# The last matrix product of a gated Fourier-mixing layer: the order of the first two units of each token block, and the memory order of two weight pieces

## The chip, the cores and the metric

One Trainium2 chip; the kernel runs on one of its cores. The metric is the device time of one execution in microseconds (us), taken as the median of several executions. Engines are called by short names: PE (TensorE: matrix products, PEld its weight loads), DVE (VectorE), ACT (ScalarE), POOL (GpSimd) and SP (SyncE, which here only issues transfers). Each engine runs its own instruction list in the order that the program wrote.

## The reference

With x of 2048 tokens by 512 features, all in 32-bit floats:

```
xn  = layernorm(x)
s   = Cseq_re @ (xn @ Cd_re.T) - Cseq_im @ (xn @ Cd_im.T)     # Fourier mixing: 2048x2048 and 512x512 matrices
h   = relu(xn @ w1 + b1) ** 2                                # 512 -> 1792
g   = silu(h @ w2 + b2)                                      # 1792 -> 512
out = x + s * g
```

The change lies in `h @ w2`, called MLP2 here.

## The kernel before, in words

**Precision and products.** Each 32-bit operand is split into a high half (HI, a rounded copy made by ACT, line 69) and a low half (LO, the remainder, subtracted by DVE, line 72), and each product is three passes: HI·HI, HI·LO, LO·HI (line 32). Matrix products of two-by-two blocks are done in the Winograd way, with seven products instead of eight (line 48). So before a product can run, its operands need sums of blocks (DVE, lines 201 to 209), then the two halves.

**Stages.** The Fourier mixing comes first; it fills the first 407 us of the span. Then MLP1 (`hidden`, line 525), and MLP2 (line 789 on). MLP1 and MLP2 are cut in 28 units each: four token blocks c = 0..3 of 512 tokens, by seven pieces p = 0..6 of the 1792 hidden features. A unit is numbered n = 7c + p; block 1 begins with unit 7, block 2 with unit 14, block 3 with unit 21. MLP1 writes each unit's h to memory (`hd`, line 557, issued on ACT's queue), and MLP2 reads it back (`hr`, line 569, on SP's queue).

**A unit of MLP2 on the engines.** `operand(n, c, p)` (line 560) loads `hr`, forms the sums on DVE (lines 207 to 209), then the HI half on ACT and the LO half on DVE into one of three places in turn (`sixth(2 + n % 3)`, line 579). `outer` (line 593) issues one product on PE: two columns of three passes, six matmuls of 128x256. A unit is seven products, 42 matmuls. In each product the first two matmuls use only the unit's HI half; the third uses its LO half.

**The weights.** w2's piece p, split and summed, has 2 halves x 7 slots x 256 columns for each partition. Pieces 0, 1 and 6 are made from w2 on the spot, late in the run. Pieces 2 to 5 lie ready in memory (`w2d`) and are loaded by `load_w2` (line 493) into places that MLP1's weights leave. Pieces 2 and 3 land where a neighbour's last 16 columns still lie, so each is loaded in two goes: "s" (slots 1 to 6 of both halves) and, when the neighbour is done, "f" (slot 0 of both halves). Piece 4 is loaded whole ("l").

**Accumulators (banks).** The seven products of a block add up in PSUM over the seven units. Products 2 and 6 share a two-bank tile, products 7, 5 and 3 a three-bank tile; 1 and 4 have a bank each. The two- and three-bank tiles are the same banks in every block, so the next block can start in them only when DVE has read out the previous block (`combine`, lines 234 to 243) and ACT has written the bias (line 591). Products 1 and 4 alternate between banks, which are free earlier. The first unit of a block therefore takes its products in the order 1, 2, 6, 4, 7, 5, 3 (`FIRST`, line 52), all other units in the order 1, 2, 6, 7, 5, 3, 4 (`ORDER`). Block 3 has an order of its own.

**What sets the order.** MLP1 and MLP2 are written under `tc.manual_schedule` (line 705): each engine executes in the order in which the Python code issues. In MLP2's loop (line 789), step n issues the products of unit n, then DVE's sums for unit n + 3, then, if it is a block's last unit, `combine`, and then the two halves of unit n + 2 (line 835) and the load of unit n + 6. So at the end of block 0 (step 6), DVE's list reads: sums of unit 9, `combine` of block 0, LO half of unit 8. In the same way the LO half of unit 15 follows `combine` of block 1.

**Counters.** A transfer tells of its landing on one of eight counters (DMAHW0 to DMAHW7), given out by the program; before a counter is used again, the issuing engine waits for the transfer that used it last.

Of the kernel before, what the change touches and what calls it, by code (L numbers as in the profile page):

```python
# [7 lines left out]
F32 = mybir.dt.float32  # L8
# [16 lines left out]
REST = NP - 3  # L25
# [24 lines left out]
ORDER = (1, 2, 6, 7, 5, 3, 4)  # L50

FIRST = (1, 2, 6, 4, 7, 5, 3)
FIRST_LAST = (1, 2, 5, 4, 6, 7, 3)
# [9 lines left out]
def fnet_gated_kernel(ctx, tc, x, xt, ct, wd, w1, w2, b1, b2, out):  # L63
    nc = tc.nc
# [22 lines left out]
    def bank(tag, name):  # L87

        n = {"b3": 3, "b2": 2}.get(tag, 1)
        return acc.tile([P, n, 512], F32, tag=tag, name=name)  # L90

    def buf(tag, shape, name, dtype=F32, bufs=1):
        return pool.tile(shape, dtype, tag=tag, bufs=bufs, name=name)
# [19 lines left out]
    def sixth(j, a, on=LINE):  # L113

        v = block[:, (7 - j) * 3584 + on:][:, 0:3584]
        return v.rearrange("p (a b n) -> p a b n", a=a, n=256)
# [189 lines left out]
    def load_rows(c, t):  # L306

        flat = rows.rearrange("a b -> (a b)")
        for m in range(2):
            for h in range(2):  # L310
                n = m * S + c * TC + h * 256
                nc.sync.dma_start(t[:, 2 * m + 1 - h], bcast(flat[n:n + 256], 256))
        xT["rows"] = t
# [138 lines left out]
    W1, W2, H, fin = {}, {}, {}, {}  # L452
# [3 lines left out]
    W2D = {p: dram.tile([P, 2, 7, 256], F32, name=f"w2d{p}") for p in range(NP) if p not in W2_DIRECT}  # L456
# [20 lines left out]
    def load_w1(p):  # L477
        if p < NP - 1:
            t = sixth(2 + p, 2)
            nc.sync.dma_start(t.bitcast(F32), W1D[p])  # L480
            W1[p] = [t[:, :, n] for n in range(7)]
        else:
            a = buf("g0b", [P, 2, 3, 256], f"w1a_{p}", F32R)
            b = buf("g1b", [P, 2, 4, 256], f"w1b_{p}", F32R)
            nc.sync.dma_start(a.bitcast(F32), W1D[p][:, :, 0:3])
            nc.sync.dma_start(b.bitcast(F32), W1D[p][:, :, 3:7])
            W1[p] = [a[:, :, n] for n in range(3)] + [b[:, :, n] for n in range(4)]

    W2_HOME = "xc0", "xc1", 5, 6, 7, "wd0", "wd1"

    FRACTION = {"l": slice(0, 7), "s": slice(1, 7), "f": slice(0, 1)}

    def load_w2(p, slots=slice(0, 7)):
        to = W2_HOME[p]
        if p not in W2:
            W2[p] = sixth(to, 2, 0) if p in (2, 3, 4) else buf(to, [P, 2, 7, 256], f"w2_{p}", F32R)
        nc.sync.dma_start(W2[p][:, :, slots].bitcast(F32), W2D[p][:, :, slots])

    def late_w2(p):

# [210 lines left out]
    def go(*names):  # L711


        for v in names:
            k, n = v[0], int(v[1:])
            if k == "m":
                load_rows(n, buf("pq00", [P, 4, 256], f"rows{n}"))
            elif k in FRACTION:
                load_w2(n, FRACTION[k])
            elif k != "h" or n < len(units):  # L720
                if v not in making:
                    making[v] = {"h": lambda: operand(n, *units[n]), "x": lambda: tokens(n // 2, n % 2),
                                 "w": lambda: late_w2(n)}[k]()
                next(making[v])
# [28 lines left out]
    c = NTC - 1  # L753
# [8 lines left out]
    with ordered:  # L762
        before = None
        for n, (c, p) in enumerate(units):
            ahead, behind = beside.get((c, p), ((), ()))
            go(*ahead)
            unit = hidden(n, c, p)
            next(unit)
            if n == 0:
                load_w1(5)  # L770
                load_w1(6)
            if n == len(units) - 1:

                m26, m4 = bank("b2", "m_b2_o0"), bank("ba", "m_ba_o0")
                bias(m26[:, 0], 2)
                bias(m4[:, 0], 4)
            if before:
                next(before)
            next(unit)
            go(*behind)  # L780
            before = unit
            if n == 0:
                stage2(NC - 1, 0)
                stage2(NC - 1, 1, "ba")
        m753, m1 = bank("b3", "m_b3_o0"), bank("bb", "m_bb_o0")
        bias(m753[:, 1], 5)
        next(before)

        for n, (c, p) in enumerate(units):
            last = c == NTC - 1  # L790
            if n == 0:
                ms = m26, m753, m4[:, 0], m1[:, 0]
                at_ = product
            elif not last and p == 0:

                m4, m26, m753, m1 = (bank(tag, f"m_{tag}_o{c}") for tag in (("bb", "ba")[c - 1], "b2", "b3", "bc"))
                ms = m26, m753, m4[:, 0], m1[:, 0]
                bias(ms[2], 4)
                bias(product(ms, 2), 2)
                bias(product(ms, 5), 5)  # L800
            elif p == 0:

                m5, m40 = (bank(tag, f"m_{tag}_last")[:, 0] for tag in ("bb", "bc"))
                m12, m67 = bank("b2", "m_12"), bank("b3", "m_67")
                m3 = bank("ba", "m_ba_last")[:, 0]
                m4 = m40, m67[:, 2]
                ms = {1: m12[:, 0], 2: m12[:, 1], 6: m67[:, 0], 7: m67[:, 1], 5: m5, 3: m3}
                at_ = dict.__getitem__
                bias(m5, 5)
                bias(m40, 4, slice(0, 1))  # L810
                bias(ms[2], 2)
                bias(m4[1], 4, slice(1, 2))

            def add(k, p):
                if last and k == 4:
                    for i in range(2):
                        outer(m4[i], k, ready[c, p], p, (i,))
                else:
                    outer(at_(ms, k), k, ready[c, p], p)

            go(*{0: ("l5",), 1: ("w6",)}.get(n, ()))
            if not last or p < REST:
                for k in ORDER if p else FIRST_LAST if last else FIRST:
                    add(k, p)
            if n == 1:

                nc.scalar.activation(stats[:, 0, 0, 0:1], stats[:, 0, 0, 0:1], AF.Silu)
            go(f"h{n + 3}")
            if p == NP - 1 and not last:
                e = buf("e", [P, 4, 512], f"z{c}")  # L830
                combine(e, ms)
                done_next = c, e
            if c and not last and p in (3, 4):
                put(*done, p - 1)
            go(f"h{n + 2}", *{2: ("w6",), 3: ("w6",)}.get(n, ()), f"h{n + 6}")
            if p == (3 if last else 5):
                load_fin(c)
            if p == NP - 1 and not last:
                done = done_next
            elif c:  # L840
                for k in ((2, 3), (0,), (1,), (), (), (), ())[p] if not last else ((), (0,), (1, 2), (3,), (), (), ())[p]:
                    finish(*done, k)


        e = buf("g1a", [P, 4, 512], f"z{c}")
        tail = NP - 1
        whole = slice(0, 512)
        w = [slice(i * 256, (i + 1) * 256) for i in range(2)]

        def rest(ks, ps=range(REST, NP)):  # L850
            for k in ks:
                for f in ps:
                    add(k, f)

        def step(to, a, b, op, w=whole):
            nc.vector.tensor_tensor(e[:, to, w], a[:, w], e[:, b, w], op=op)

        rest((1, 2, 6), range(REST, tail))
        rest((1, 2), (tail,))
        nc.scalar.activation(e[:, C21], ms[1], AF.Copy)  # L860
        step(C11, ms[2], C21, ALU.add)
        silu(e, C11)
        times(c, e, C11)
        plus(c, e, C11)
        rest((6,), (tail,))
        rest((7,))
        step(C22, ms[6], C21, ALU.add)
        step(C21, ms[7], C22, ALU.subtract)
        rest((5,))
        step(C12, m5, C22, ALU.subtract)  # L870
        step(C22, m5, C21, ALU.add)
        silu(e, C22)
        rest((3,))
        for f in range(REST, NP):
            outer(m4[0], 4, ready[c, f], f, (0,))
        times(c, e, C22)
        plus(c, e, C22)
        step(C12, m3, C12, ALU.add)
        silu(e, C12)
        step(C21, m4[0], C21, ALU.subtract, w[0])  # L880
        silu(e, C21, one)
        for f in range(REST, NP):
            outer(m4[1], 4, ready[c, f], f, (1,))
        times(c, e, C12)
        step(C21, m4[1], C21, ALU.subtract, w[1])
        silu(e, C21, two)
        times(c, e, C21, one)
        plus(c, e, C21, one)
        times(c, e, C21, two)
        plus(c, e, C21, two)  # L890
        plus(c, e, C12)
# [43 lines left out]
```

## Time and profile before

| | |
|---|---|
| median of 3 executions | 707.4 us (706.16 to 708.9) |
| the profiled execution | 707.11 us, of which 705.3 us are the span of its instructions |
| PE busy | 685.6 us, 97% |
| DVE busy | 583.9 us, 83% |
| ACT busy | 346.7 us, 49% |
| bytes moved | 141.09 MB, 200 GB/s mean |
| MLP2 on PE | from 553.18 us to the end |

Timeline rows read: start, length, engine, source line, operation, what it writes and reads, count; in brackets the engine's idle time just before and what ended it. `m_bb_o`, `m_b_o`, `m_ba_o`, `m_bc_o` are accumulator banks of MLP2; the `m_b_o` stand for both the two-bank and the three-bank tile. `block` is the large area that holds the units' halves and the weights. The views give line 598 for every product of MLP2 and line 72 for every LO half, so a unit is known by its place in the order.

### The profile page before, as it was taken

What the parts mean: (1) busy time and instruction counts of PE and PEld (TensorE: products, weight loads), DVE (VectorE), ACT (ScalarE), POOL (GpSimd) and SP (SyncE); (2) the same over time, 40 slices, a digit from 0 to 9 for tenths busy, and PEclk for the clock granted to TensorE, in tenths of its full rate; (3) what the DMA queues carried; (4) which work ended last, traced back from release to release, by engine and by line L of the source; (5) the groups of instructions that cost most, each with busy time, mean ns of one, the idle gap of its engine ahead of it and who ended that gap; (6) DMA issues with size and microseconds to landing.
All of it is one profiled execution on the core that took longest, in us unless ns stands there. A gap on an engine that the chain in (4) does not pass through costs nothing.

```text
span 705.3 us, 12798 instructions
## 1 busy us (share of the span) xinstructions
PE 685.6 (97%) x5179; PEld 646.1 (92%) x5179; DVE 583.9 (83%) x886; ACT 346.7 (49%) x475; POOL 5.2 (1%) x8
## 2 busy tenths in 40 slices
PE   8999999999999999999999999999999988999985
PEld 5778788999999999999999989999999988999985
DVE  7999654779599698797797756999999679999995
ACT  3447332444353544544452415777777744444531
POOL 0000000000000000000000000000000000101000
PEclk9999999999999999999999999999999999999999
DMA  9622441534563653835836976566737985777733
GB/s 323 229 90 91 153 131 46 196 119 141 203 226 135 221 200 119 299 132 179 293 99 251 357 299 210 207 234 216 269 122 235 356 334 180 194 224 193 248 125 123
DMA packets 55818, 141.09 MB, mean 200 GB/s; under 512 B 5072, under 2 KB 22224, under 8 KB 54736
## 3 DMA queue, kind: packets, MB, share of 16 engines
q1 hardware_dynamic: 50640, 124.56, 51.1%
q10 hardware_dynamic: 4032, 14.68, 5.2%
q0 software_dynamic: 1088, 1.05, 1.1%
q8 instruction: 40, 0.66, 0.4%
q14 instruction: 18, 0.15, 0.1%
HBM read 97.00 MB, written 43.27 MB: 199 GB/s over the span
## 4 chain that ended last, share of the span: by engine, by line
PE 73%; DVE 18%; DMA 4%; issue 2%; ACT 1%; SPq 0%; DVEq 0%; ACTq 0%
PE m_b L300 23%; PE yps L287 12%; PE hps L544 7%; PE m_b_o L598 7%; PE m_bb L300 5%; PE m_ba L300 5%; PE hps_b L544 4%; DVE block L72 4%; PE pq_b L353 3%; PE hps_ba L544 2%; DVE g L72 2%; DMA w2raw<-in_w 1%; DVE bn L133 1%; PE m_bc_o L598 1%; PE hps_bb L544 1%
## 5 line engine op out<-in xcount | busy, mean ns | idle before, releaser
L300 PE MATMUL m_b<-g,block 128*128 128x256 f32 x1080 | 129.1, 276 | 0.0
L300 PEld LDWEIGHTS m_b<-g,block 128*128 128x128 f32 x1080 | 125.5, 188 | 0.0
L69 ACT ACTIVATE g<-r 128x768 fp32r<-128x768 f32 (+2 forms) x65 | 57.3, 885 | 82.8 <-PE m_b L300 38.1
L72 DVE TENSOR_TENSOR g<-r,g 128x768 fp32r<-128x768 f32 (+2 forms) x65 | 65.4, 1007 | 35.3 <-ACT g L69 35.2
L287 PE MATMUL yps<-wd,pq 128*128 128x512 f32 (+1 forms) x414 | 92.9, 374 | 0.0
L287 PEld LDWEIGHTS yps<-wd,pq 128*128 128x128 f32 x414 | 74.8, 188 | 14.0
L72 DVE TENSOR_TENSOR g<-t,g 128x1024 fp32r<-128x1024 f32 x48 | 58.6, 1221 | 11.8 <-ACT g L69 11.8
L544 PE MATMUL hps<-xT,block 128*128 128x256 f32 x504 | 59.7, 277 | 0.7 <-DVE h L243 0.7
L544 PEld LDWEIGHTS hps<-xT,block 128*128 128x128 f32 x504 | 58.4, 188 | 1.0 <-PE hps L544 0.9
L69 ACT ACTIVATE g<-t 128x1024 fp32r<-128x1024 f32 x48 | 50.3, 1048 | 14.4 <-PE m_ba L300 6.5
L353 PE MATMUL pq_b<-g,block 128*128 128x512 f32 x180 | 47.6, 398 | 1.8 <-DVE g L72 1.7
L598 PE MATMUL m_b_o<-w,block 128*128 128x256 f32 x360 | 43.7, 277 | 2.6 <-ACT m_b_o L591 2.6
L555 ACT ACTIVATE h<-h,b1s 128x512 f32<-128x512 f32 x56 | 37.3, 715 | 17.3 <-DVE h L242 17.2
L300 PE MATMUL m_b<-g,xc 128*128 128x256 f32 x360 | 45.1, 277 | 0.0
L598 PEld LDWEIGHTS m_b_o<-w,block 128*128 128x128 f32 x360 | 42.0, 188 | 3.3 <-ACT m_b_o L591 3.2
L69 ACT ACTIVATE block<-hr 128x768 fp32r<-128x768 f32 (+1 forms) x28 | 35.5, 1269 | 18.6 <-DVE hr L209 7.7
L353 PEld LDWEIGHTS pq_b<-g,block 128*128 128x128 f32 x180 | 32.9, 188 | 11.3 <-DVE g L72 2.4
L300 PEld LDWEIGHTS m_b<-g,xc 128*128 128x128 f32 x360 | 42.9, 188 | 0.3
L72 DVE TENSOR_TENSOR block<-hr,block 128x768 fp32r<-128x768 f32 (+1 forms) x28 | 41.6, 1485 | 0.1
L201 DVE TENSOR_TENSOR t<-r 128x512 f32<-128x512 f32 x48 | 32.9, 685 | 4.9 <-DMA r<-in_ct 4.7
L544 PE MATMUL hps_b<-xT,block 128*128 128x256 f32 x288 | 34.7, 276 | 0.0
L544 PEld LDWEIGHTS hps_b<-xT,block 128*128 128x128 f32 x288 | 33.6, 188 | 0.0
(200 smaller groups left out, 1182.1 us busy)
## 6 DMA issues: line engine op xcount, KB each, us to landing
r<-in_ct SPq DMA_DIRECT2D x63, 512.0 KB, 3.6
hd<-h ACTq DMA_DIRECT2D x28, 512.0 KB, 4.7
hr<-hd SPq DMA_DIRECT2D x28, 512.0 KB, 4.9
w1d<-w0g SPq DMA_DIRECT2D x21, 512.0 KB, 3.2
block<-w1d SPq DMA_DIRECT2D x6, 1792.0 KB, 8.7
y<-ysb SPq DMA_DIRECT2D x16, 256.0 KB, 3.0
fin<-y SPq DMA_DIRECT2D x16, 256.0 KB, 4.8
out<-z SPq DMA_DIRECT2D x15, 256.0 KB, 4.0
```

What stands on the lines that cost most here:

```text
L69: nc.scalar.activation(hi, src, AF.Copy)
L72: return nc.vector.tensor_tensor(lo, src, hi.bitcast(F32), op=ALU.subtract)
L133: nc.vector.bn_stats(bn, t[:, h])
L201: nc.vector.tensor_tensor(t[:, 0:2], r[:, 0:1].to_broadcast([P, 2, 256]), r[:, 1:3], op=ALU.add)
L287: nc.tensor.matmul(ps[:, s], PQ[c, m, k // 2][:, a_, w:w + P], WD[m, k][:, b_, s], start=n == 0, stop=n > len(todo) - 3, skip_group_check= ...
L300: nc.tensor.matmul(ps[:, d * CW:(d + 1) * CW], w[:, a_, d * P:(d + 1) * P], mv(b_), start=first and d == 0 and (a_, b_) == (HI, HI), stop= ...
L353: nc.tensor.matmul(accs[c][k], w, g[:, b_, 2 * h:2 * h + 2], start=j == 0 and h == 0 and (a_, b_) == (HI, HI), stop=j == NJ - 1 and h == 1 ...
L544: nc.tensor.matmul(product(ms, k), W1[p][a][:, a_, q * P:(q + 1) * P], xT[c, q][:, b_, b], start=share not in first, stop=q == 1 and (a_, ...
L555: nc.scalar.activation(x_[:, s], x_[:, s], AF.Relu, bias=b1s[:, f:f + 1])
L598: nc.tensor.matmul(m[:, k * 256:(k + 1) * 256], g[:, a_, a, k * P:(k + 1) * P], W2[p][:, b_, b], start=p == 0 and k == 0 and (a_, b_) == ( ...
```

## The change

It has two parts.

*The order on PE.* In blocks 0, 1 and 2, the first two units are interleaved. The products of both units on the alternating banks come first: 1, 2, 6, 4 in block 0 (where the two-bank tile is free too), 1 and 4 in blocks 1 and 2; first for the block's first unit, then for its second. Then the first unit's other products, then the second's. Block 3 keeps its order. What DVE, ACT and POOL execute, and in which order, does not change.

*The weight pieces.* The 2 x 7 x 256 of a piece are now taken as one row of 3584 columns. "f" is its first 256 columns (slot 0 of HI alone), "s" the remaining 3328 (all the rest, LO's slot 0 among it). Each is one contiguous range for a partition; before, each was two ranges that lay between those of the other.

```
-    FRACTION = {"l": slice(0, 7), "s": slice(1, 7), "f": slice(0, 1)}
+    FRACTION = {"l": slice(0, 3584), "s": slice(256, 3584), "f": slice(0, 256)}
...
-        nc.sync.dma_start(W2[p][:, :, slots].bitcast(F32), W2D[p][:, :, slots])
+        to, src = (v.rearrange("p a b n -> p (a b n)")[:, which] for v in (W2[p], W2D[p]))
+        nc.sync.dma_start(to.bitcast(F32), src)
...
-            if not last or p < REST:
-                for k in ORDER if p else FIRST_LAST if last else FIRST:
+            if last:
+                if p < REST:
+                    for k in ORDER if p else FIRST_LAST:
+                        add(k, p)
+            elif p == 0:
+                early = (1, 4) if c else (1, 2, 6, 4)
+                for k in early:
+                    add(k, 0)
+            elif p == 1:
+                for k in early:
+                    add(k, 1)
+                for f in (0, 1):
+                    for k in ORDER:
+                        if k not in early:
+                            add(k, f)
+            else:
+                for k in ORDER:
                     add(k, p)
```

On PE, at the start of block 1, the program had these rows (`m_bc_o` is product 1, `m_b_o_6409` products 2 and 6, `m_bb_o` product 4, `m_b_o_6410` products 7, 5 and 3; `w_0` marks the block's first unit, number 7, and `w_1` its second, number 8):

```order
986 L598 MATMUL m_bc_o_6411<-w_0_5647,block 128x256 x6
987 L598 MATMUL m_b_o_6409<-w_0_5647,block 128x256 x12
988 L598 MATMUL m_bb_o_6408<-w_0_5647,block 128x256 x6
989 L598 MATMUL m_b_o_6410<-w_0_5647,block 128x256 x18
990 L598 MATMUL m_bc_o_6411<-w_1_5829,block 128x256 x6
991 L598 MATMUL m_b_o_6409<-w_1_5829,block 128x256 x12
992 L598 MATMUL m_b_o_6410<-w_1_5829,block 128x256 x18
993 L598 MATMUL m_bb_o_6408<-w_1_5829,block 128x256 x6
```

Unit 8's first product stood behind all seven of unit 7. In the changed program the same place on PE reads:

```order
986 L599 MATMUL m_bc_o_6411<-w_0_5647,block 128x256 x6
987 L599 MATMUL m_bb_o_6408<-w_0_5647,block 128x256 x6
988 L599 MATMUL m_bc_o_6411<-w_1_5829,block 128x256 x6
989 L599 MATMUL m_bb_o_6408<-w_1_5829,block 128x256 x6
990 L599 MATMUL m_b_o_6409<-w_0_5647,block 128x256 x12
991 L599 MATMUL m_b_o_6410<-w_0_5647,block 128x256 x18
992 L599 MATMUL m_b_o_6409<-w_1_5829,block 128x256 x12
993 L599 MATMUL m_b_o_6410<-w_1_5829,block 128x256 x18
```

Unit 8's products 1 and 4 moved ahead of five products of unit 7; they stand behind two.

On SP's list, in the last units of MLP1, the two pieces of weights 2 (`w2d_923`) and 3 (`w2d_924`) stood between loads of `hr`, with these waits before (DMAHW counters, and PE or DVE for a place to come free):

```order
194 L497 DMA block<-w2d_923 128x2x256 [waits DMAHW6_49,PE_49]
195 L497 DMA block<-w2d_924 128x2x1536 [waits DMAHW3_49,PE_49]
196 L569 DMA hr_4_5894<-hd_4_931 128x1024 [waits DMAHW4_49]
197 L497 DMA block<-w2d_924 128x2x256 [waits DMAHW3_49,PE_49]
198 L569 DMA hr_3_5954<-hd_3_930 128x1024 [waits DMAHW5_49,DMAHW7_49,DMAHW1_49,Activation_49]
```

In rows 194 and 197 the counter is that of the same weights' larger piece, so the small one waited for the large one to land. The changed program has in the same place on SP:

```order
194 L498 DMA block<-w2d_923 128x256 [waits PE_49]
195 L498 DMA block<-w2d_924 128x3328 [waits DMAHW3_49,PE_49]
196 L570 DMA hr_4_5894<-hd_4_931 128x1024 [waits DMAHW4_49]
197 L498 DMA block<-w2d_924 128x256 [waits DMAHW5_49,PE_49]
198 L570 DMA hr_3_5954<-hd_3_930 128x1024 [waits DMAHW6_49,DMAHW1_49,Activation_49]
```

The order is the same; the small pieces no longer wait for the large ones (DMAHW5 in row 197 was last used by an earlier `hd`), and the counters that follow are dealt out otherwise.

On ACT's list, at the end of MLP1, this is unit 25's store of h (`hd_4`) and what stands behind it, before:

```order
380 L557 DMA hd_4_952<-h_4_5879 128x1024 [waits Activation_49]
381 L69 ACTIVATE block<-hr_1_5652 128x1792 [waits DMAHW3_49,DVE_49]
382 L549 ACTIVATE h_6_6003<-hps_1_5960 128x256 [waits DMAHW7_49,PE_49]
383 L591 ACTIVATE m_b_o_6005<-b2s 128x512 [waits DVE_49]
387 L557 DMA hd_5_953<-h_5_5941 128x1024 [waits DMAHW1_49,Activation_49]
```

`hd_5` waited for the `hd` of two units earlier. The changed program has on ACT:

```order
380 L558 DMA hd_4_952<-h_4_5879 128x1024 [waits DMAHW0_49,Activation_49]
381 L69 ACTIVATE block<-hr_1_5652 128x1792 [waits DMAHW3_49,DVE_49]
382 L550 ACTIVATE h_6_6003<-hps_1_5960 128x256 [waits DMAHW7_49,PE_49]
383 L592 ACTIVATE m_b_o_6005<-b2s 128x512 [waits DVE_49]
387 L558 DMA hd_5_953<-h_5_5941 128x1024 [waits DMAHW4_49,Activation_49]
```

`hd_4` now waits on a counter that was last used by the load of `hr` of unit 2 (row 193 of SP), and `hd_5` on that of `hr_4` (row 196 of SP).

More of the change, by code (lines that the diff above doesn't have):

```diff
@@ L489, in fnet_gated_kernel, with load_w2 @@
     W2_HOME = "xc0", "xc1", 5, 6, 7, "wd0", "wd1"
-    FRACTION = {"l": slice(0, 7), "s": slice(1, 7), "f": slice(0, 1)}
-    def load_w2(p, slots=slice(0, 7)):
+    FRACTION = {"l": slice(0, 3584), "s": slice(256, 3584), "f": slice(0, 256)}
+    def load_w2(p, which):
         to = W2_HOME[p]
```

## The prediction

> **What bounds the kernel now.** I read the page first, then the timelines of PE and DVE at the points where MLP2's blocks begin. PE is busy for 97% of the span, so nearly all it can lose or win lies in a few waits. In MLP2 the PE timeline shows these, with the rows around them:
>
> ```profile
> 557.07 2.32 PE L598 MATMUL m_b_o<-w,block 128*128 128x256 f32 x18 [1.00 <-ACT m_b_o L591]
> ...
> 563.98 0.39 PE L598 MATMUL m_bb_o<-block 128*128 128x256 f32 x2
> 566.91 1.22 PE L598 MATMUL m_bb_o<-block 128*128 128x256 f32 x4 [2.54 <-DVE block L72]
> ...
> 592.56 0.84 PE L598 MATMUL m_bc_o<-w,block 128*128 128x256 f32 x6
> 594.71 1.65 PE L598 MATMUL m_b_o<-w,block 128*128 128x256 f32 x12 [1.30 <-ACT m_b_o L591]
> ...
> 597.36 2.31 PE L598 MATMUL m_b_o<-w,block 128*128 128x256 f32 x18 [0.32 <-ACT m_b_o L591]
> 599.50 0.84 PE L598 MATMUL m_bc_o<-w,block 128*128 128x256 f32 x6
> 600.18 3.56 PE L598 MATMUL m_b_o<-w,block 128*128 128x256 f32 x30
> ...
> 604.26 0.84 PE L598 MATMUL m_bc_o<-block 128*128 128x256 f32 x6
> ...
> 684.28 0.73 PE L598 MATMUL m<-w,block 128*128 128x256 f32 x4 [2.37 <-DVE block L72]
> ```
>
> Unit 8 runs from 599.50 to 604.26, so a unit costs 4.76 us, a product 0.68 us, a matmul 0.113 us. The waits of 1.00 (block 0) and 1.30 and 0.32 us (block 1) are for banks; they are what the new order aims at. The wait of 2.54 us is for unit 2's LO half; in it PE had done two matmuls (x2) and stood at the third. PE runs its matmuls in order: whoever comes too early holds up all behind.
>
> The second view is DVE's timeline, at the same two block starts:
>
> ```profile
> 592.80 1.22 DVE L240 TENSOR_TENSOR z<-m_b_o,z 128x1024 f32<-128x1024 f32 x1
> ...
> 597.32 1.22 DVE L72 TENSOR_TENSOR block<-hs,block 128x1024 fp32r<-128x1024 f32 x1
> 598.45 0.95 DVE L72 TENSOR_TENSOR block<-hr,block 128x768 fp32r<-128x768 f32 x1
> ...
> 627.58 1.22 DVE L241 TENSOR_TENSOR z<-m_b_o,z 128x1024 f32<-128x1024 f32 x1 [0.75 <-PE m_b_o L598]
> ...
> 631.91 0.95 DVE L72 TENSOR_TENSOR block<-hr,block 128x768 fp32r<-128x768 f32 x1
> ...
> 661.06 1.23 DVE L241 TENSOR_TENSOR z<-m_b_o,z 128x1024 f32<-128x1024 f32 x1 [0.69 <-PE m_b_o L598]
> ```
>
> The rows at 597.32 and 598.45 are unit 8's LO half, in two instructions; they come behind the four steps of `combine` (592.80 on) and end at 599.40. PE starts unit 8 at 599.50. Unit 15's LO half ends at 631.91 + 0.95 = 632.86. So the second unit of a block is ready only when the block has run for one unit's length; today that costs nothing. DVE is hardly ever idle, and in each `combine` it waits for PE (0.75 and 0.69): there the two are tied.
>
> **Part 1, the new order, block 1.** PE would do unit 7's products 1 and 4 (2 x 0.68, until 593.92), then two matmuls of unit 8 (0.23), and stand at 594.15 until unit 8's LO half is there, at 599.40: a stall of 5.25 us. The front's shift, below, moves DVE and PE alike and is counted there. What is left then is four matmuls of product 1 (0.45), product 4 (0.68), and five products of each unit (10 x 0.68): 7.93 us, until 607.33. Before, unit 8 was done at 604.26. So block 1 loses 3.07 us. The 1.62 us of bank waits vanish, since the banks are free by 597.36, but they vanish inside a longer wait. Nothing hides the loss: behind the stalled matmul stand all of PE's products, and `combine` of block 1 waits for PE already.
>
> **Block 2.** Before, unit 13 ended at 628.06 and unit 15 at 637.74, 9.68 us later:
>
> ```profile
> 628.06 0.84 PE L598 MATMUL m_bc_o<-w,block 128*128 128x256 f32 x6
> ...
> 637.74 0.84 PE L598 MATMUL m_bc_o<-block 128*128 128x256 f32 x6
> ```
>
> DVE's step at 627.58 waits for PE, and from there to unit 15's LO half is DVE's own work, so that half is ready 632.86 - 628.06 = 4.80 us after PE has finished block 1, whenever that is. PE reaches the third matmul of unit 15 after 1.36 + 0.23 = 1.59 us, stalls 3.21 us, and needs 7.93 us more: 12.73 instead of 9.68, a loss of 3.05 us. Block 3 is not interleaved. Its chain hangs on `combine` of block 2, which waits for PE (661.06), then on DVE, for which PE waits at 684.28. So both losses reach the end: +6.1 us.
>
> **The clock.** The windows view shows the clock granted to PE (the last number but two) around the wait of 2.54 us:
>
> ```profile
> 545.00:553.00 8.00, 8.00 (x73) 8.00 (x72) 7.52 (x13) 5.86 (x10) 0.00 (x0) 1.00 0.97 329
> 553.00:564.00 11.00, 10.00 (x89) 9.80 (x88) 5.35 (x9) 8.46 (x11) 0.00 (x0) 1.00 1.02 385
> 564.00:567.00 3.00, 0.47 (x5) 0.27 (x3) 2.93 (x4) 1.79 (x2) 0.00 (x0) 0.96 1.01 423
> 567.00:573.00 6.00, 6.00 (x40) 6.00 (x41) 5.69 (x9) 1.80 (x2) 0.00 (x0) 0.74 1.01 424
> ...
> 662.00:698.00 36.00, 33.57 (x292) 32.98 (x290) 31.64 (x43) 13.06 (x16) 0.00 (x0) 1.00 0.51 170
> ```
>
> A mean of 0.96 over 3 us and 0.74 over 6 us is half clock for 0.24 + 3.12 = 3.4 us, that is 1.7 us of PE lost; the wait of 2.37 us in the last stretch cost none. Stalls of 5.25 and 3.21 us are longer than the one that did, so I add 1.7 us for each: +3.4. The bounds are 0 (as at 2.37) and two such periods each.
>
> The Trainium skill, "TensorE: Matmul & The Clock Gate" (HAM oscillation), says to avoid PE gaps above about 3.4 us, since the clock falls after an idle window of that length that is not tied to the kernel's start. The trace disagrees on the length: 2.54 us were enough once. By the page the second stall would cost nothing; that is the first rival.
>
> **Part 2, the weight pieces, and what they do to the front.** SP's waits, DVE's idle time and the transfers at the end of MLP1:
>
> ```profile
> SPq L497 <- DMA block<-w2d: 10.1, 2, 6.8
> ```
> ```profile
> 563.31 0.69 DVE L207 TENSOR_TENSOR hs<-hr 128x512 f32<-128x512 f32 x1 [5.47 <-DMA hr<-hd]
> ...
> 577.38 0.69 DVE L201 TENSOR_TENSOR w2raw<-w2raw 128x512 f32<-128x512 f32 x1 [3.22 <-DMA w2raw<-in_w]
> ```
>
> SP loses its two waits (10.1 us), `hr` of unit 3 is issued earlier, and DVE's idle 5.47 us shrinks. But what sets DVE from 577.38 on is the load of weights 6, far back in the same queue. DVE works without a pause from there through block 0's `combine`:
>
> ```profile
> 593.00:605.00 12.00, 10.38 (x89) 9.98 (x88) 11.65 (x14) 6.09 (x7) 1.23 (x1) 1.00 0.57 183
> ```
>
> So the front gains what this load gains. The transfers were busy all along (0.97 to 1.02 above) and the same bytes must pass, but at 329 and 385 GB/s, against 424 later. At 424 the stretch 545 to 564 (8 x 329 + 11 x 385 = 6870 kB) would take 16.2 instead of 19 us. The best case is thus -2.8 us; if earlier issue only queues, 0. I take -1.8, nearer the best, because SP's waits go and the small pieces have half as many ranges.
>
> One cost stands against it. ACT's `hd_4` now waits for the load of unit 2's `hr`. Behind it on ACT stand unit 1's HI half and the biases.
>
> ```profile
> 545.06 0.33 SPq L569 DMA_DIRECT2D hr<-hd  x1
> ```
> ```profile
> 549.58 0.36 ACTq L557 DMA_DIRECT2D hd<-h  x1
> ```
> ```profile
> hr<-hd SPq DMA_DIRECT2D x13, 512.0 KB, 6.0
> ```
>
> With the median of 6.0 us that load lands at 551.1, so ACT stands about 1.5 us, and unit 1's and 2's halves come later by as much. In block 0 four products of each unit can run before the three-bank tile is needed (8 x 0.68 = 5.4 us from 553.18), which covers it, and DVE still has 3.22 us in hand before weights 6. I cost it at nothing; without that cover it is +1.5. The 1.00 us of bank wait in block 0 goes, and so, in part, does the wait of 2.54; both lie ahead of DVE's chain and buy nothing more.
>
> **The sum.** From the profiled execution, 707.1 us (its 705.3 us of span and the 1.8 us around it stay as they are; the median of the runs is 0.3 higher): +3.07 +3.05 +3.4 -1.8 = +7.7, **714.8 us**.
>
> **The rivals.**
> - *The clock falls once.* If only a gap well above 3.2 us lets it fall, block 2's stall keeps full clock: 714.8 - 1.7 = 713.1. For it: 2.37 us did no harm, so it isn't length alone; against it: 2.54 us did.
> - *The clock holds at both.* 714.8 - 3.4 = 711.4, and 710.4 with the front's best bound. Against it the same row.
> - *The front gains nothing.* The transfers share one pool that is busy already; issue moves, landing doesn't: 714.8 + 1.8 = 716.6. For it: the shares of 0.97 to 1.02. The Trainium skill, "DMA: Bandwidth & Descriptors" (Issuing engines are not separate DMA queues), says that all issuers' transfers run on the same 16 engines and interleave, so other issuing saves only issue time, which is this rival.
> - *The front gets later.* ACT's new waits add 1.5 us to DVE's chain: 707.1 + 6.1 + 3.4 + 1.5 = 718.1. Against it: DVE's 3.22 us in hand.
> - *Faster.* The second unit's LO half does not hold PE, and PE arrives early enough at both `combine`s that DVE's 0.75 and 0.69 us go, with the front at its best: 707.1 - 2.8 - 1.4 = 702.9. This decides on one point: units 8's and 15's LO halves would have to be ready within 1.6 us of their block's start, not 6.8 and 4.8 us after it. Against it: DVE's order is unchanged, with `combine` ahead of them.
>
> **How the numbers follow.** About 0.5%, 3.5 us, is what can be told from no change here. Chances: forecast 0.42 (714.8), clock once 0.20 (713.1), front nothing 0.13 (716.6), clock holds 0.15 (711.4; 0.09 of it with the best front, within 3.5 us), front later 0.05 (718.1), faster 0.05 (702.9). Slower by over 0.5%: 0.42 + 0.20 + 0.13 + 0.06 + 0.05 = 0.86; same 0.09; faster 0.05. The range goes from the clock holding with the best front to between the two late fronts: 710.4 to 717.4; it leaves out faster, front later and part of the clock case.
>
> **What would show it.** Right: waits on PE at products of `m_bc_o` behind DVE's line-72 rows, about 5.2 us in block 1 and 3.2 us in block 2, half clock after each; bank waits for ACT gone; the load of weights 6 lands about 1.8 us earlier. Wrong: unit 8's LO half ahead of `combine`; or no such stalls; or a loss in block 0, behind ACT's `hd_4`.

## The result and the profile after

| | before | after |
|---|---|---|
| median, first comparison (4 runs each) | 708.15 us (706.16 to 709.5) | 716.37 us (713.47 to 717.66) |
| the profiled execution | 707.11 us, span 705.3 | 717.66 us, span 715.9 |
| PE busy | 685.6 us | 689.7 us |

The changed kernel is slower: the ratio is 1.0092, with a 95% interval of 1.0069 to 1.0116. The forecast was 714.8 us.

PE's timeline in blocks 1 and 2 of the changed kernel. `m_bc_o` is the bank of product 1 of a block's first two units; their product 4 goes to `m_bb_o` in block 1:

```profile
592.18 0.39 PE L599 MATMUL m_bc_o<-w,block 128*128 128x256 f32 x2
597.72 1.16 PE L599 MATMUL m_bc_o<-w,block 128*128 128x256 f32 x4 [5.15 <-DVE block L72]
...
599.96 7.81 PE L599 MATMUL m_b_o<-w,block 128*128 128x256 f32 x60
607.61 0.87 PE L599 MATMUL m_bc_o<-block 128*128 128x256 f32 x6
...
632.34 0.87 PE L599 MATMUL m_bc_o<-w,block 128*128 128x256 f32 x6
...
633.76 0.40 PE L599 MATMUL m_bc_o<-w,block 128*128 128x256 f32 x2
637.17 0.74 PE L599 MATMUL m_bc_o<-w,block 128*128 128x256 f32 x4 [3.02 <-DVE block L72]
638.45 7.23 PE L599 MATMUL m_b_o<-w,block 128*128 128x256 f32 x60
645.52 0.87 PE L599 MATMUL m_bc_o<-block 128*128 128x256 f32 x6
```

In both blocks PE does two matmuls of the second unit (x2), stops at the third for 5.15 and 3.02 us, and the 60 matmuls behind it wait along. Unit 8 ends at 607.61 (604.26 before), unit 15 at 645.52 (637.74 before).

DVE's timeline of the same execution says what PE waits for. The first row is the point at which weights 6 have arrived:

```profile
575.65 0.69 DVE L201 TENSOR_TENSOR w2raw<-w2raw 128x512 f32<-128x512 f32 x1 [3.06 <-DMA w2raw<-in_w]
...
591.07 1.22 DVE L240 TENSOR_TENSOR z<-m_b_o,z 128x1024 f32<-128x1024 f32 x1
592.39 1.23 DVE L241 TENSOR_TENSOR z<-m_b_o,z 128x1024 f32<-128x1024 f32 x1
593.65 1.22 DVE L242 TENSOR_TENSOR z<-m_b_o,z 128x1024 f32<-128x1024 f32 x1
594.98 0.69 DVE L243 TENSOR_TENSOR z<-m_ba_o,z 128x512 f32<-128x512 f32 x1
595.59 1.22 DVE L72 TENSOR_TENSOR block<-hs,block 128x1024 fp32r<-128x1024 f32 x1
596.72 0.95 DVE L72 TENSOR_TENSOR block<-hr,block 128x768 fp32r<-128x768 f32 x1
```

Unit 8's LO half (595.59 and 596.72) comes behind the four steps of `combine`, without a pause between. It ends at 597.67 and PE goes on at 597.72. Weights 6 are there 1.73 us earlier than before (575.65 against 577.38), and so is the LO half (597.67 against 599.40).

The windows view of the same execution around the two stalls and the last wait; the last number but two is the clock granted to PE:

```profile
597.00:600.00 3.00, 2.28 (x11) 2.28 (x12) 2.93 (x5) 1.22 (x3) 0.00 (x0) 0.64 0.56 175
600.00:605.00 5.00, 5.00 (x39) 5.00 (x39) 3.78 (x6) 0.84 (x1) 1.33 (x1) 0.88 0.47 121
634.00:637.00 3.00, 0.15 (x2) 0.00 (x0) 2.90 (x4) 2.59 (x4) 0.00 (x0) 1.00 0.45 180
637.00:641.00 4.00, 3.83 (x32) 3.83 (x33) 3.93 (x7) 0.76 (x2) 0.00 (x0) 1.00 0.04 4
690.00:698.00 8.00, 5.66 (x35) 5.46 (x34) 6.13 (x8) 1.79 (x2) 0.00 (x0) 0.79 0.87 269
```

After block 1's stall the clock was at half for 3 x 0.36 x 2 + 5 x 0.12 x 2 = 3.4 us. After block 2's it was not, but it was for another 8 x 0.21 x 2 = 3.4 us around block 3's wait, which is no longer than before (2.34 us; 2.37 before).

### The profile page after: what moved, and what is told of

Read it like the earlier page. It is cut to its first block, busy times and chain, and to the rows that moved or that the text cites. A ratio compares the mean times of both kernels' runs of the same rounds, so it can differ in the third digit from the quotient of the medians.

```text
span 715.9 us, 12793 instructions
## 1 busy us (share of the span) xinstructions
PE 689.7 (96%) x5179; PEld 650.4 (91%) x5179; DVE 584.7 (82%) x886; ACT 346.8 (48%) x475; POOL 5.2 (1%) x8
## 4 chain that ended last, share of the span: by engine, by line
PE 73%; DVE 18%; DMA 4%; issue 3%; ACT 1%; SPq 0%; DVEq 0%; ACTq 0%
PE m_b L300 23%; PE yps L287 12%; PE m_b_o L599 7%; PE hps L545 7%; PE m_bb L300 5%; PE m_ba L300 5%; DVE block L72 4%; PE hps_b L545 4%; PE pq_b L353 3%; PE hps_ba L545 2%; DVE g L72 2%; DMA hr<-hd 2%; DMA w2raw<-in_w 1%; PE m L599 1%; DVE bn L133 1%
```

## The experiments

Theory T: the second unit's LO half stands behind `combine` on DVE, so the two stalls, with the half clock that follows some of them, are the loss; the new layout gives back what weights 6 gain. The rivals: the layout itself costs (R1) or does nothing (R2); the order costs wherever it stands; the loss is one of pace and the stalls only show it. Ratios are to the kernel before, run on the same chip; us are such a ratio's distance from 1 (or from another ratio) times 709.

**The order alone.** The weight pieces stay as they were.

```
-    FRACTION = {"l": slice(0, 3584), "s": slice(256, 3584), "f": slice(0, 256)}
+    FRACTION = {"l": slice(0, 7), "s": slice(1, 7), "f": slice(0, 1)}
```

> The new order of the products on PE and the new banks stay, the weight pieces lie interleaved in memory as before, so the changed front of MLP2's weight load is gone. Theory T (the second unit's LO half on DVE stands behind combine, PE stalls on it in blocks 1 and 2; the pieces give some 1.7 us back): 1.7 us slower than after, about 10 us slower than before (718), with waits of about 5 us and 3 us on PE for DVE's LO halves. Rival R1 (the new layout of the weight pieces is what costs the time): within 1 us of before. Rival R2 (the layout does nothing at all): the same as after, 8 to 9 us slower than before, and unit 8's LO half ends at the same time as in after's profile, 597.7.

Measured: 718.47 us, ratio 1.0135 (1.0113 to 1.0157). The waits on PE from 420 us on:

```profile
PE m_bc_o L598 <- DVE block L72: 6.2, 2, 3.1
PE m_bb_o L598 <- DVE block L72: 5.9, 1, 5.9
```

Columns: sum, count, longest. The layout is not what costs; R1 falls. Block 1's wait is 3.1 and not the expected 5 us, since a 5.9 us wait for unit 2's LO half has already made PE late in block 0. With the layout of after, that wait is 1.56 us.

**The layout alone.** The order of before.

```
+            if not last or p < REST:
+                for k in ORDER if p else FIRST_LAST if last else FIRST:
+                    add(k, p)
-            if last:
...
-            elif p == 0:
-                early = (1, 4) if c else (1, 2, 6, 4)
...
```

> Only the weight pieces' layout of the change, with the order of products and banks of before. T: 1 to 2 us faster than before (706.5), since weights 6 land and unit 8's LO half ends 1.7 us earlier, as in after's profile. R1 (the layout costs): slower than before by 2 us or more. R2 (the front gains nothing because PE or a bank is late anyway): within 0.5 us of before.

Measured: 706.85 us, ratio 0.9978 (0.9965 to 0.9991), that is -1.6 us (-2.5 to -0.6). R2 falls. Two rows, of DVE and of PE:

```profile
576.30 0.69 DVE L201 TENSOR_TENSOR w2raw<-w2raw 128x512 f32<-128x512 f32 x1 [3.17 <-DMA w2raw<-in_w]
```
```profile
559.62 3.47 PE L599 MATMUL m_b_o<-w,block 128*128 128x256 f32 x18 [2.97 <-ACT m_b_o L592]
```

Over all the profiles, DVE's step at line 201 starts at 574.50 to 576.30 in the nine with the new layout (mean 575.5) and at 577.19 to 577.53 in the three with the old one (mean 577.4): 1.9 us. The second row is the price of ACT's new counter waits, a bank wait of 2.97 us in block 0 (1.00 before). It lies ahead of DVE's wait for weights 6, and costs nothing at the end.

**Interleaving in block 0 only.**

```
+            elif c:
+                for k in ORDER if p else FIRST:
+                    add(k, p)
             elif p == 0:
```

> The layout of after and the interleaved order in block 0 only; blocks 1 and 2 keep the order of before. T: the same as the run with the layout alone within 0.7 us, so 1 to 2 us faster than before; no wait over 2 us on PE in blocks 1 and 2, none of 5.15. A rival by which the interleaved order costs wherever it stands (half the matmuls at another bank, ACT's longer wait ahead of its store): slower than the layout alone by 2 us or more.

Measured: 707.2 us, ratio 0.9981 (0.9964 to 0.9998): the same as the layout alone. The bank wait of 2.97 us is gone in its trace, and that gains nothing. Where no `combine` stands ahead of the second unit, interleaving costs and gains nothing that these intervals could tell.

**The LO halves ahead of `combine`.** After, with both halves of the block's second unit issued ahead of `combine` in steps 6 and 13. This moves the LO half on DVE, and on ACT the HI half, ahead of `combine`'s one step there (line 239). PE's order and banks stay as in after.

```
+            sooner = p == NP - 1 and c < NTC - 2
+            if sooner:
+                go(f"h{n + 2}")
...
-            go(f"h{n + 2}", *{2: ("w6",), 3: ("w6",)}.get(n, ()), f"h{n + 6}")
+            if not sooner:
+                go(f"h{n + 2}")
+            go(*{2: ("w6",), 3: ("w6",)}.get(n, ()), f"h{n + 6}")
```

> After, with one edit: in blocks 1 and 2 the second unit's HI and LO halves are issued on DVE ahead of the block's combine. T: the 5.15 us and 3.02 us waits on PE fall below 1 us, the half clock after the first goes, and the time comes to 706 to 710, within 2 us of before. A rival by which the order or the slower pace of matmuls is the loss and the waits only show it: 714 or more, near after.

Measured: 706.64 us, ratio 0.9979 (0.9963 to 0.9994). DVE and PE at the start of block 1:

```profile
590.55 1.22 DVE L72 TENSOR_TENSOR block<-hs,block 128x1024 fp32r<-128x1024 f32 x1
591.69 0.95 DVE L72 TENSOR_TENSOR block<-hr,block 128x768 fp32r<-128x768 f32 x1
592.55 1.22 DVE L240 TENSOR_TENSOR z<-m_b_o,z 128x1024 f32<-128x1024 f32 x1
```
```profile
592.68 0.87 PE L599 MATMUL m_bc_o<-w,block 128*128 128x256 f32 x6
593.38 0.87 PE L599 MATMUL m_bb_o<-w,block 128*128 128x256 f32 x6
594.46 1.68 PE L599 MATMUL m_b_o<-w,block 128*128 128x256 f32 x12 [0.21 <-ACT m_b_o L592]
597.11 5.71 PE L599 MATMUL m_b_o<-w,block 128*128 128x256 f32 x48 [0.97 <-ACT m_b_o L592]
```

The LO half now ends at 592.64 with `combine` behind it, and PE takes unit 8's products without a stop; what is left is 0.21 and 0.97 us of bank waits. The whole loss of after is gone with this change of order. Its part on ACT is an unlikely cause, since in after that HI half was done at 589.46 and no wait on PE was for it; what PE waited for is DVE's LO half. Order and pace as the loss fall with it.

**One block at a time.** Block 1 takes the order of before; in the second kernel block 2 does, with `c == 2` in the first line.

```
+            elif c == 1:
+                for k in ORDER if p else FIRST:
+                    add(k, p)
             elif p == 0:
```

> After, with block 1 in the order of before and blocks 0 and 2 interleaved. T (each interleaved block with a combine in it costs its own stall on PE): block 1's 5.15 us wait goes with the half clock behind it, block 2's wait of about 3 us stays. Against the 706.85 us of the layout alone that is one stall of 3.0, so 709.9 us, or 711.6 us if the clock falls behind it this time. Rival (the stall of block 2 is only a late effect of block 1's delay, or the loss is one of pace): 707 us or, for pace, as after, about 715.

> After, with block 2 in the order of before and blocks 0 and 1 interleaved. T: block 1's wait of 5.2 us stays and costs 3.1 us net, with the half clock behind it 1.7 more; against the layout alone that is 706.85 + 4.8 = 711.6 us. Rival (the delay of block 1 is absorbed at the next wait for DVE, since unit 15's LO half is then the one that ends last): 707 to 708 us.

Measured: without block 1, 712.22 us, ratio 1.0049 (1.003 to 1.0068); without block 2, 712.7 us, ratio 1.0054 (1.0032 to 1.0075). The stalls that are left, in the first kernel and in the second:

```profile
631.24 0.94 PE L599 MATMUL m_bc_o<-w,block 128*128 128x256 f32 x4 [3.10 <-DVE block L72]
```
```profile
598.13 1.23 PE L599 MATMUL m_bc_o<-w,block 128*128 128x256 f32 x4 [4.93 <-DVE block L72]
```

Each block costs by itself. Against block 0 alone (0.9981, on another chip), block 2 costs 0.0068, or 4.8 us, and block 1 costs 0.0073, or 5.2 us, each within some 2 us; neither is a late effect of the other.

**The LO halves ahead, and the remaining products by bank.** The fourth kernel, and:

```
-                for f in (0, 1):
-                    for k in ORDER:
-                        if k not in early:
-                            add(k, f)
+                for ks in ((2, 6), (7, 5, 3)):
+                    for f in (0, 1):
+                        for k in ks:
+                            if k not in early:
+                                add(k, f)
```

> The run with the LO halves issued ahead of combine, and with the first two units' remaining products taken bank by bank, so that the first unit's first bank is finished earlier and ACT empties it while PE does the second half. T: no wait over 1 us on PE in MLP2's blocks 1 and 2, 1 us less than with the LO halves ahead alone: 705 to 706 us. Rival (combine, which is now later, and the units behind it set the pace, not the banks): the same as the LO halves ahead alone, 706.6 us, or later by up to 1 us.

Measured: 705.56 us, ratio 0.9951 (0.9935 to 0.9966). This is the fastest version of all, 0.34 to 0.65% below before. PE at the start of block 1:

```profile
593.79 0.74 PE L599 MATMUL m_bc_o<-w,block 128*128 128x256 f32 x4 [0.65 <-DVE block L72]
...
595.56 7.08 PE L599 MATMUL m_b_o<-w,block 128*128 128x256 f32 x60 [0.34 <-ACT m_b_o L592]
```

**Control: the LO halves ahead, in the order of before.** The fourth kernel's edit, with the second kernel's, which keeps the layout of after and puts the order of products of before back:

```
+            if not last or p < REST:
+                for k in ORDER if p else FIRST_LAST if last else FIRST:
+                    add(k, p)
-            if last:
...
```

> Control: the order of products and banks of before, the weight layout of after, and the LO halves issued ahead of combine. If the interleaving is worth anything once its stall is gone, this is slower than the run with both (706.6 us): combine is then some 2 us later, and the waits on PE for a bank that before's profile shows return in blocks 1 and 2 with 1.6 us or more each, 708 to 711 us. Rival (issuing the LO halves earlier gives a gain of its own that the interleaving only hides): 705 us or less.

Measured: 709.12 us, ratio 1.0001 (0.9982 to 1.002). The wait for a bank in block 1 doubles, from 1.30 to 2.67 us; in block 2, where one was expected too, none came:

```profile
594.34 1.63 PE L599 MATMUL m_b_o<-w,block 128*128 128x256 f32 x12 [2.67 <-ACT m_b_o L592]
```

So the interleaving does what it is for once its stall is gone: 0.9951 with it (by bank) against 1.0001. With the products of the fourth kernel, not yet by bank, it is 0.9979 against 1.0001, and the intervals still overlap.

**The changed kernel again**, unedited, and **the fastest version with the old layout** (the first experiment's edit on the seventh):

> The changed kernel again, unedited, for a closer ratio and for the granted clock of more runs. T with the terms added up as the single runs give them (block 1 alone and block 2 alone cost 5.2 and 4.8 us against the run with only block 0 interleaved): 707.2 + 10 = 717 us if the two add up whole, 1.012 of before; 715 us (1.009) if the clock falls behind one of the two stalls only. Under 713 us the stalls would hide in one another.

> The fastest version so far (LO halves ahead of combine, the remaining products bank by bank) with the weight pieces interleaved in memory as before. T (the layout of the pieces gives 1 to 2 us wherever weights 6 set DVE's chain): 1 to 2 us slower than with the layout of after, 706.5 to 708 us. Rival (the layout gains nothing once the stalls are gone): 705.5 us.

Measured: the changed kernel 716.65 us, ratio 1.0113 (1.0092 to 1.0134). The fastest version with the old layout 707.8 us, ratio 0.9983 (0.9962 to 1.0003), so the layout is worth 0.0032, or 2.3 us, there as well, though the intervals just overlap.

What the new order and the early LO halves are worth together is less sure than what the layout is. Against the layout alone (0.9978, 0.9965 to 0.9991) the fastest version is 0.0027, or 1.9 us, ahead, on another chip and with intervals that touch; with the old layout both together come to 0.9983, and the interval includes 1.

The clock after the two stalls, in the second profile of the changed kernel:

```profile
595.00:603.00 8.00, 6.42 (x32) 6.42 (x33) 7.57 (x11) 2.08 (x3) 1.33 (x1) 0.57 0.43 131
635.00:640.00 5.00, 4.00 (x21) 4.01 (x22) 4.93 (x9) 1.59 (x3) 0.00 (x0) 0.66 0.21 42
```

This time it fell at both: 8 x 0.43 x 2 = 6.9 us of half clock by these rounded means at the first, from within the stall on, and 5 x 0.34 x 2 = 3.4 us at the second.

## Why the prediction was right

*Block 1, forecast +3.07.* Right. By the forecast's own steps unit 8 ends at 604.26 - 1.8 + 3.07 + 1.7 = 607.2; it ended at 607.61. Alone the block cost 5.2 us, against 3.07 + 1.7 = 4.8.

*Block 2, forecast +3.05.* Right. From unit 13's end to unit 15's it took 645.52 - 632.34 = 13.18 us, against 12.73, without half clock but with slower matmuls (below). Alone the block cost 4.8 us, against 3.05 + 1.7 = 4.75. With some 2 us of uncertainty, the two costs of single blocks hardly tell a stall with half clock from one without; the stalls themselves are read from the profiles: 5.15 and 4.94 us in block 1 (forecast 5.25), 3.02 and 3.10 us in block 2 (forecast 3.21).

*The front, forecast -1.8.* Right: -1.73 us in the profile, -1.9 as a mean over the profiles, -1.6 us in the time of the layout alone. The size was a choice between 0 and -2.8, so that it came so close is in part luck. The rival by which only issue time is saved falls. Before weights 6 the transfers ran faster, in the windows of the changed kernel:

```profile
545.00:553.00 8.00, 8.00 (x73) 8.00 (x72) 7.21 (x13) 5.55 (x8) 0.00 (x0) 1.00 0.99 368
553.00:563.00 10.00, 10.00 (x89) 9.94 (x89) 6.93 (x11) 7.21 (x10) 0.00 (x0) 1.00 0.99 406
```

Before it was 329 and 385 GB/s, at shares as high. What moved the rate, the earlier issue or the longer ranges, was not separated. One reading of the forecast was too wide, without harm to its sum: DVE waits for PE in the `combine` of blocks 1 and 2 (0.75 and 0.69 us), not in each; in block 0 it goes from one to the next without a pause.

*The clock, forecast +3.4.* Mis-sized, and tied too firmly to the two stalls. In the changed kernel's two profiles it fell after block 1's stall both times, after block 2's once, and once after block 3's wait, for which the forecast had none; that the first profile has two periods, as forecast, is luck. Over its ten runs the mean granted clock is 0.9899, over the 17 runs of before in the second comparison 0.9929. As an estimate, with PE taken as busy throughout, that is 0.0101 x 716.5 - 0.0071 x 709.3 = 7.2 - 5.0 = +2.2 us. With the runs of before beside the other experiments (0.9933 and 0.9937) it is up to +2.8 us. The mean also counts half clock behind the last matmul, which costs nothing (in the first profiles the last 2.0 us of the span, with and without the change), so this is rough.

*ACT's new waits, costed at nothing.* Right in the sum, wrong in the place. The forecast priced `hd_4` at 1.5 us. ACT's timeline:

```profile
548.91 1.06 ACT L557 ACTIVATE h<-h 128x1024 f32<-128x1024 f32 x1
550.34 0.33 ACTq L558 DMA_DIRECT2D hd<-h  x1
...
555.04 1.06 ACT L557 ACTIVATE h<-h 128x1024 f32<-128x1024 f32 x1
557.99 0.33 ACTq L558 DMA_DIRECT2D hd<-h  x1
558.42 0.60 ACT L592 ACTIVATE m_b_o<-b2s 128x512 f32<-128x512 f32 x1 [2.32 <-DVE hr L208]
```

`hd_4` stood 550.34 - 549.97 = 0.4 us; `hd_5`, which was not priced, stood 557.99 - 556.10 = 1.9 us, since the counter that it shares belongs to the load of `hr_4`, which was issued at 546.83 and landed 11.1 us later, at 557.9. The bias of a bank (558.42) stands behind it and comes 2.0 us later than before (556.41). The view names DVE for this wait, but the step that it names ends at 558.10, when `hd_5` had been issued already. In the order of before (the layout alone) the late bias became the bank wait of 2.97 us; in the new order block 0 has work on other banks meanwhile, as argued.

*The sum.* +3.07 + 3.05 + 2.2 - 1.8 = +6.5 us, or 7.1 with the clock at 2.8, where 8.2 us (first comparison) and 8.0 us (second, 0.0113 x 709) were measured. The interval of either is about 1.5 us wide on each side. What is left, 0.9 to 1.7 us, may be the pace that comes next; in runs without a profile it can't be seen, so this stays open.

## What to carry to other kernels

When an engine runs strictly in order, work brought forward is only as early as its latest operand: before the order of the products is changed, follow each operand back to its engine and look for what stands ahead of it there. Here the remedy for the banks and the order of DVE's list belonged together. All with the new layout, which by itself came to 0.9978: the new order alone lost (1.0113), the early LO halves alone gained nothing (1.0001), and both, with the products taken bank by bank, came to 0.9951. A wait that the change leaves on another engine is harmless only while something later sets the pace, and the row to check is that later one (here the arrival of weights 6).

## What the runs showed of the hardware

**The clock fell after gaps far shorter than expected, and by their position.** PE in the kernel with the LO halves ahead, in block 0:

```profile
565.13 1.09 PE L599 MATMUL m_bb_o<-block 128*128 128x256 f32 x4 [1.56 <-DVE block L72]
566.02 4.92 PE L599 MATMUL m_b_o<-block 128*128 128x256 f32 x30
...
572.18 3.70 PE L599 MATMUL m_b_o<-block 128*128 128x256 f32 x30
...
603.34 3.56 PE L599 MATMUL m_b_o<-block 128*128 128x256 f32 x30
```
```profile
565.00:569.00 4.00, 3.87 (x19) 3.88 (x20) 3.93 (x7) 3.01 (x4) 0.00 (x0) 0.57 1.05 443
```

A wait of 1.56 us was followed by 4 x 0.43 x 2 = 3.4 us of half clock (30 matmuls in 4.92 us instead of 3.56). Length does not decide: waits of 1.56 us here, 2.34 (after, block 3), 2.54 (before) and 5.15 us were followed by half clock, but not the same 1.56 us in the fastest version, nor 2.37 (before, block 3), 3.02 (after, block 2) and 3.10 us (the order alone, block 1). Each period in MLP2 lasted about 3.4 us, or went on for a second one. So where a gap falls in time decides as much as how long it is. The windows view of the changed kernel's first profile shows it when it is cut at the length of a period (3.413 us in the trace); the number behind the length is PE's busy time:

```profile
594.41:597.83 3.42, 0.11 (x1) 0.11 (x1) 3.32 (x5) 2.86 (x4) 0.00 (x0) 1.00 0.23 75
597.83:601.24 3.41, 3.41 (x16) 3.41 (x17) 3.34 (x5) 0.39 (x1) 0.00 (x0) 0.50 0.46 151
635.37:638.79 3.42, 1.62 (x13) 1.62 (x14) 3.35 (x6) 2.39 (x4) 0.00 (x0) 1.00 0.03 12
638.79:642.20 3.41, 3.41 (x31) 3.41 (x30) 3.41 (x5) 0.08 (x1) 0.59 (x1) 1.00 0.32 91
689.99:693.40 3.41, 1.07 (x9) 0.87 (x8) 3.34 (x5) 1.79 (x2) 0.00 (x0) 1.00 0.71 227
693.40:696.81 3.41, 3.41 (x18) 3.41 (x17) 2.80 (x4) 0.00 (x0) 0.00 (x0) 0.50 0.98 285
```

The two periods of half clock begin 95.57 us apart, 28 times that length, and in every profile all periods lie on such a grid, with another offset in each. Over the twelve profiles, from 20 us on, all 28 windows of the grid at full clock in which PE was busy for less than 1.45 us (12 of them at the kernel's end) were followed by half clock, 2 of the 16 with 1.45 to 1.9 us, and none of the 2335 with more. Block 2's stall of 3.02 us was spread over two windows with 2.19 and 1.62 us busy, and nothing followed; the one of 3.10 us in the second profile fell in one window (0.49 us busy), and half clock followed. As an estimate from these counts, a stall of 5 us always brings half clock, and one of 3.1 us does in about three of four places on the grid. These are counts, not an experiment: no run shifted a stall on purpose.

The Trainium skill, "TensorE: Matmul & The Clock Gate" (Part 1: The HAM clock gate), describes a window of 3.4 us that runs free of the kernel, which these rows agree with. They do not agree with the condition of the same part, a whole idle window: waits of 1.56 us here and of 1.55 us in the run without block 1 were enough. Two executions of one kernel differ in this (the changed kernel's block 2: none, then 3.4 us), so half clock after a short gap is to be priced with a chance.

**A matmul takes 0.113 or 0.118 us at the same granted clock.** In the rows above, 30 matmuls took 3.70 us at 572.18 and 3.56 us at 603.34, both at full clock:

```profile
572.00:576.00 4.00, 4.00 (x36) 4.00 (x36) 0.96 (x3) 1.31 (x1) 0.00 (x0) 1.00 0.94 383
603.00:607.00 4.00, 4.00 (x38) 4.00 (x37) 3.93 (x6) 2.33 (x3) 0.30 (x2) 1.00 0.79 154
```

Such stretches are 10 to 70 us long, lie at other places in each execution, of kernel before too, and mostly begin or end where a stall ends or a block begins. In the changed kernel's first profile one ran from 601 to 674 us (60 matmuls in 7.23 us, against 6.96): 73 x 4% = 2.9 us. That may be why this execution took 717.66 us at a mean granted clock of 0.994, where another of the four took 713.47 us at 0.996; the others have no profile. The cause of the slower pace is open.
